# Stored attention outputs in a pool of their own, and the last batch's low halves on VectorE, in a three-stage attention and mixture kernel

## The chip, the cores and the metric

The kernel runs on one core of one Trainium2 chip. The metric is the device time of one execution in microseconds (us). A core has TensorE (PE, matmuls and transposes), VectorE (DVE), ScalarE (ACT), GpSimd (POOL) and SyncE (SP), which here only issues DMA transfers. Each engine runs its own instructions in their order and waits at semaphores for the others. The profile shows the TensorE clock as the share of full speed that was granted.

## The reference

Three blocks follow each other for 8 batches of 576 tokens, 512 features wide, all in float32.

```
phi(x)  = [exp(xw - max|xw|), exp(-(xw - max|xw|))]         # xw = x @ w_phi, per head
attn    = phi(q) @ (phi(k)^T @ v) / (phi(q) @ sum(phi(k)))  # 8 heads of 64
# mixture: 4 experts, the best 2 of 4 by gate logits, weights by softmax
y      += w_e * softmax(causal(q_e k_e^T / 8)) v_e @ wo_e
# second mixture block, x_prev is x one token earlier
xk, xr  = mu_k x + (1 - mu_k) x_prev,  mu_r x + (1 - mu_r) x_prev
out     = sigmoid(xr @ w_r) * ((relu(xk @ w_k)^2) @ w_v)
```

## The kernel before

**Number form.** A float32 matrix product is made of three matmuls in a reduced form (fp32r): each operand is split into a high half (a rounded copy, on ACT) and a low half (operand minus high half, on DVE or POOL); the products are high x high, high x low and low x high. `split` (lines 95 to 100; the subtraction is line 100) and `mm3` do that.

**Stages.** `favors` makes the attention of all batches into the buffer XT. `moe1` takes a batch from XT, makes queries, keys, values and gates, and runs the causal attention of 4 experts in tasks of 128 queries: scores, softmax (POOL's scaling is line 558), transposes, product with the values (`av_task`, tile yp, summed into `yf`). After two experts, `taps` (lines 611 to 622) makes the *stored attention output* of that batch and half: `dl` is the difference of neighbouring tokens, and the tile `yt` holds high and low halves of the even tokens (288 columns) and of the differences (576 columns). ACT makes the high halves, `el` the low ones, and SP stores all of it (864 KB) to `yd` in DRAM. So `taps` runs 16 times.

`gates_keys` reads `yd` back in 6 chunks of 768 tokens and multiplies it by weights that were composed with `wo` beforehand (`compose`; its results pass through a tile in the same buffer as `yt`): 36 units a chunk, 6 matmuls each (tile rk), evacuated by ACT or DVE, stored to `kd`. The weights of a unit (tile wt, 256 KB) are loaded by SP into one of 5 buffers, asked for when the unit four places earlier is evacuated.

`moe2` is the last product. It reads a chunk of `kd` as four blocks b11, b12, b21, b22 and makes it in 7 products instead of 8 (the sums T1 = b12 - b11, T2 = b22 - T1, T3 = b22 - b12, T4 = b21 - T2). Each block is split into one of three slots of XT, then 24 matmuls follow (tile vacc, two halves of 12). `post` gathers the products: the third and fourth are kept as `u2` and `u4` until the sixth and seventh, and the gates (tile zs, sigmoid on ACT) multiply the output.

**Order.** `weave` interleaves the streams and a scheduler sets each engine's order when the kernel is built. The first `weave` ends with `moe1`; then the pools of that stage are closed (`phA.close()`), and the PSUM pool psB and the SBUF pool pB of the last stage are opened. Pools at the right side lie on each other as in a stack: XT, pQ (four weight tiles, used again as buffers later), then pA, and after pA is closed, pB in the room that pA had. A tile of pB waits until the tiles of pA that lay there are no longer read or written. The first two products of chunk 0 (b11, b21) need nothing of pB: their blocks are loaded to XT and pQ and split there by `first`. The raw b11 stays in `wqh` and `wql`, and b12 and b22 in XT, until lines 866 to 869 make the sums from them in pB.

The condition in line 618 asks for a key 'pW' in `state`; the code puts 'pW' in `late` alone, so `el` is POOL for all 16.

Of the kernel before, what the change touches and what calls it, by code (L numbers as in the profile page):

```python
# [6 lines left out]
F32 = mybir.dt.float32  # L7
F32R = mybir.dt.float32r
# [5 lines left out]
P = 128  # L14
B, S, H, D = (8, 576, 8, 64)
# [8 lines left out]
HP_ = S // 2  # L24
HC = CH // 2
# [51 lines left out]
def fused_kernel(ctx: ExitStack, tc: tile.TileContext, qT, kT, vx, wphi, wq, wk, wvg, wo, mu, w64, ident, cmask, tri, out):  # L77
# [14 lines left out]
    def eng(c):  # L92
        return {'v': nc.vector, 'p': nc.gpsimd}[c]
# [13 lines left out]
    state = {}  # L107
# [16 lines left out]
    XT = pX.tile([P, 16 * S], F32R, name='XT')  # L124
    pQ = ctx.enter_context(tc.tile_pool(name='pQ', bufs=1, side='right'))
    wqh, wql, wkh, wkl = (pQ.tile([P, 2, 4, P], F32R, name=n) for n in ('wqh', 'wql', 'wkh', 'wkl'))
    pA = phA.enter_context(tc.tile_pool(name='pA', bufs=1, side='right'))
    phF = ExitStack()
    pF = phF.enter_context(tc.tile_pool(name='pF', bufs=1))
# [77 lines left out]
    def compose():  # L207
        sw = [pR.tile([P, 4, 256], F32R, name='sw', tag=f'y{h}') for h in range(2)]
        for i in range(2):
            st_ = pR.tile([P, 2, 256], F32, name='wof', tag='e', bufs=4)  # L210
            nc.sync.dma_start(st_, wo[:, 2 * i:2 * i + 2])
            split(sw[0][:, 2 * i:2 * i + 2], sw[1][:, 2 * i:2 * i + 2], st_)
            yield 1
        for u in range(12):
            wth, wtl = ([pR.tile([P, 2, 2, P], F32R, name=n, tag='w', bufs=NWB) for _ in range(2)] for n in ('wth', 'wtl'))
            for hf in range(2):
                hz = (yield from decode(pF, 2 * u + hf, dict(tag='e', bufs=4), 'a', pool_raw=pR))
                hz = hz.rearrange('p (k n) -> p k n', k=2)
                a_ = pF.tile([P, 2, P], F32, name='ma', tag='dr')
                for k in range(2):  # L220
                    nc.vector.tensor_scalar(a_[:, k], hz[:, k], mus[:, int(u < 4), 2 * hf + k:2 * hf + k + 1], None, op0=OP.mult)
                split(wth[hf][:, :, 0], wtl[hf][:, :, 0], hz, 'a', nc.gpsimd)
                yield 1
                split(wth[hf][:, :, 1], wtl[hf][:, :, 1], a_, 'a', nc.gpsimd)
                yield 1
            ps = psK.tile([P, 512], F32, name='fo', tag='rk')
            for ep in range(2):
                es = slice(ep * P, ep * P + P)
                mm3(ps[:, ep * 256:ep * 256 + 256], [(sw[0][:, kt, es], sw[1][:, kt, es], wth[kt // 2][:, kt % 2].rearrange('p x n -> p (x n)'), wtl[kt // 2][:, kt % 2].rearrange('p x n -> p (x n)')) for kt in range(4)])
                yield 1  # L230
            f_ = pF.tile([P, 2, 2, P], F32, name='cb', tag='pm', bufs=3)
            o = pA.tile([P, 2, 3, 2, P], F32R, name='wo_', tag='yt')
            p4 = ps.rearrange('p (e x n) -> p e x n', e=2, x=2)
            evac('a', f_[:, 0], p4[:, :, 0])
            oh, ol = (o[:, h].rearrange('p x e n -> p e x n')[:, :, 0::2] for h in range(2))
            evac('a', oh, p4)
            nc.vector.tensor_sub(f_[:, 1], p4[:, :, 1], f_[:, 0])
            nc.vector.tensor_sub(ol, p4, oh.bitcast(F32))
            split(o[:, 0, 1], o[:, 1, 1], f_[:, 1], 'a', nc.gpsimd)
            nc.sync.dma_start(wf[u], o.bitcast(F32))  # L240
            yield 1
        state['composed'] = True
# [174 lines left out]
    def moe1():  # L417
# [167 lines left out]
        def av_task(b, e, hf):  # L585
            ep, j = (e // 2, e % 2)
            W = 256 if hf == 0 else 320
            q0 = 256 * hf
            d = {}
            hr = slice(64 * j, 64 * j + 64)  # L590

            def mm():
                ps = psA.tile([P, 320], F32, name='yp', **tg('yp'))
                hi, lo = (x.rearrange('p (k q) -> p k q', q=W) for x in AT[b, e, hf])
                nk = 2 if hf == 0 else 5
                cost = 0
                for pa, (cw, src) in enumerate(((P, hi), (64, lo))):
                    for k in range(nk):
                        o = max(0, P * k - q0)
                        nc.tensor.matmul(ps[:cw, o:W], VS[b][:, k, e, :cw], src[:, k, o:W], start=pa == 0 and k == 0, stop=pa == 1 and k == nk - 1, skip_group_check=True)  # L600
                        cost += max((W - o) / 2.4, cw / 1.2)
                d['ps'] = ps
                return cost

            def ev():
                ps = d['ps']
                yc = pA.tile([64, 320], F32, name='yc', tag='a', bufs=3)
                evac('a', yc[:, :W], ps[64:P, :W])
                nc.vector.tensor_add(YF[ep][hr, 1 + q0:1 + q0 + W], ps[0:64, :W], yc[:, :W])

            def taps():
                if not (j == 1 and hf == 1):
                    return
                yf = YF[ep]
                dl = pA.tile([P, S], F32, name='dl', tag='a', bufs=3)
                nc.vector.tensor_sub(dl, yf[:, 1:], yf[:, 0:S])
                yt = pA.tile([P, 2, 3, HP_], F32R, name='yt', tag='yt')
                el = eng('v' if 'pW' in state else 'p')
                split(yt[:, 0, 0], yt[:, 1, 0], yf[:, 1:].rearrange('p (t two) -> p two t', two=2)[:, 0], 'a', el)
                split(yt[:, 0, 1:], yt[:, 1, 1:], dl.rearrange('p (t two) -> p two t', two=2), 'a', el)  # L620
                nc.sync.dma_start(yd[b][:, :, ep], yt.bitcast(F32))
                stored[b] = stored.get(b, 0) + 1
            return [mm, ev, taps]
# [169 lines left out]
    late = {}  # L793

    def moe2():
# [33 lines left out]
        def chunk(c):  # L829
            pB = late['pB']  # L830
            d = {}

            def load(*names):

                def go():
                    for n in names:
                        if n == 'w2':
                            d[n] = combo(2, 0, 2, pB, pB, 1536, 'kx', 8)
                        elif n[0] == 'w':
                            d[n] = home(int(n[1]), *((wkh, wkl) if n == 'w5' else (wqh, wql)))  # L840
                        elif n[0] == 'g':
                            d[n] = pB.tile([P, 4, HC], F32, name='zs', tag='zs', bufs=2)
                            nc.sync.dma_start(d[n], kd[c][:, 0:4, int(n[1])])
                        elif n[0] == 'b':
                            d[n] = pB.tile([P, 4, HC], F32, name='kx', tag='kx', bufs=8)
                            nc.sync.dma_start(d[n], block(c, *src[n], 0, 4))
                return (lambda: done.get(c, 0) >= (NB if 'g0' in names else 24), go)
# [60 lines left out]
            def post(j):  # L908
# [7 lines left out]
                def tmp(tag, bufs):  # L916
                    return pB.tile([P, HC], F32, name='t', tag=tag, bufs=bufs)

                def go():
                    for dp in range(2):  # L920
                        x, y, w = (d.get((k, dp)) for k in 'xyw')
                        g = lambda par, r: d[f'g{par}'][:, 2 * dp + r]
                        if j == 0:
                            d['z', dp] = tmp('t', 3)
                            evac('a', d['z', dp], x)
                        elif j == 1:
                            nc.vector.tensor_add(out_(dp, 0)[:, 0], y, d['z', dp])
                        elif j == 2:
                            d['u2', dp] = tmp('u2', 2)
                            evac('a', d['u2', dp], x)  # L930
                        elif j == 3:
                            d['u4', dp] = tmp('u4', 2)
                            evac('a', d['u4', dp], x)
                        elif j == 4:
                            o = out_(dp, 0)[:, 0]
                            nc.vector.tensor_mul(o, o, g(0, 0))
                            nc.vector.tensor_mul(out_(dp, 0)[:, 1], x, g(1, 0))
                            store(dp, 0)
                        else:
                            t = tmp('t', 3)  # L940
                            nc.vector.tensor_add(t, w, d['u4' if j == 5 else 'u2', dp])
                            nc.vector.tensor_mul(out_(dp, 1)[:, 6 - j], t, g(6 - j, 1))
                            if j == 6:
                                store(dp, 1)
# [84 lines left out]
```

## Time and profile before

| | |
|---|---|
| median of 3 runs | 1256.39 us (1253.61 to 1257.29) |
| profiled execution | 1252.4 us, span 1250.4 us |
| mean granted clock | 0.992 |
| PE busy | 1210.9 us (97%) |
| DVE busy | 938.9 us (75%) |
| ACT busy | 817.9 us (65%) |
| POOL busy | 434.2 us (35%) |
| chain that ended last | PE 81%, DVE 7%, DMA 4%, ACT 3% |

PE is busy nearly all the time, so the profile is read for the stretches in which it is not. In the page's strip of forty slices of 31 us the PE share is under nine tenths in four slices (the first, those from 813 and 1000 us on, and the last), and the granted clock in two of them (the first, and the one from 1000 us on). "Idle before" at a row of an engine names the time that it stood still and what released it.

### The profile page before, as it was taken

What the parts mean: (1) busy time and instruction counts of PE and PEld (TensorE: products, weight loads), DVE (VectorE), ACT (ScalarE), POOL (GpSimd) and SP (SyncE); (2) the same over time, 40 slices, a digit from 0 to 9 for tenths busy, and PEclk for the clock granted to TensorE, in tenths of its full rate; (3) what the DMA queues carried; (4) which work ended last, traced back from release to release, by engine and by line L of the source; (5) the groups of instructions that cost most, each with busy time, mean ns of one, the idle gap of its engine ahead of it and who ended that gap; (6) DMA issues with size and microseconds to landing.
All of it is one profiled execution on the core that took longest, in us unless ns stands there. A gap on an engine that the chain in (4) does not pass through costs nothing.

```text
span 1250.4 us, 26664 instructions
## 1 busy us (share of the span) xinstructions
PE 1210.9 (97%) x9014; PEld 1169.7 (94%) x9014; DVE 938.9 (75%) x2489; ACT 817.9 (65%) x2008; POOL 434.2 (35%) x634
## 2 busy tenths in 40 slices
PE   8999999999999999999999999989999989999998
PEld 7899899999999999999999999988898879999998
DVE  7875988888977777787788678747667577767765
ACT  6665767677767776776668667568577575456533
POOL 5542666445633334553544543333113200000000
PEclk8999999999999999999999999999999989999999
DMA  6322134322226444454555434755798988798753
GB/s 203 93 88 85 62 103 149 109 71 80 101 96 181 131 133 118 114 172 137 150 141 185 127 118 125 221 197 171 231 296 265 324 295 284 247 315 300 270 192 127
DMA packets 186918, 212.70 MB, mean 170 GB/s; under 512 B 34464, under 2 KB 170528, under 8 KB 186784
## 3 DMA queue, kind: packets, MB, share of 16 engines
q1 hardware_dynamic: 172960, 192.12, 49.2%
q10 hardware_dynamic: 13824, 18.88, 4.2%
q8 instruction: 73, 1.20, 0.4%
q14 instruction: 61, 0.50, 0.1%
HBM read 145.94 MB, written 65.01 MB: 169 GB/s over the span
## 4 chain that ended last, share of the span: by engine, by line
PE 81%; DVE 7%; DMA 4%; ACT 3%; issue 2%; POOL 2%; SPq 0%; POOLq 0%; ACTq 0%; DVEq 0%
PE rk L117 16%; PE vacc L903 13%; PE kv L342 9%; PE num L385 8%; PE qk L117 6%; PE vp L117 4%; PE yp L600 3%; PE at L565 3%; PE pj L287 3%; PE pj L288 2%; PE pj L289 2%; PE tq L369 2%; PE fo L117 2%; PE sc L527 2%; PE sc L528 2%
## 5 line engine op out<-in xcount | busy, mean ns | idle before, releaser
L558 POOL TENSOR_SCALAR a<-a,sv,gw 128x128 f32<-128x128 f32 (+4 forms) x160 | 108.1, 677 | 222.8 <-DVE sv L552 79.6
L100 POOL TENSOR_TENSOR lo<-raw,hi 128x256 fp32r<-128x256 f32 (+1 forms) x160 | 110.0, 690 | 180.5 <-ACT hi L97 167.6
L385 PE MATMUL num<-kvs,ph 128*128 128x65 f32 (+1 forms) x1280 | 142.2, 262 | 0.6 <-DVE xs L392 0.6
L385 PEld LDWEIGHTS num<-kvs,ph 128*128 128x128 f32 (+1 forms) x1280 | 137.2, 181 | 4.5 <-issue 1.3
L903 PE MATMUL vacc<-XT,wch 128*128 128x384 f32 x480 | 124.2, 337 | 2.6 <-DVE XT L100 2.5
L297 DVE TENSOR_REDUCE m<-pj 128x4 f32<-128x512 f32 (+1 forms) x160 | 100.8, 631 | 34.1 <-PE pj L289 32.8
L547 ACT ACTIVATE a<-sc,sv 128x128 f32<-128x128 f32 (+2 forms) x192 | 98.1, 513 | 20.5 <-DVE sv L542 11.5
L740 DVE TENSOR_TENSOR z<-rk,z 128x384 f32<-128x384 f32 x144 | 79.1, 551 | 36.0 <-PE rk L117 29.5
L299 DVE TENSOR_TENSOR pm<-pj,m 128x512 f32<-128x512 f32 (+1 forms) x160 | 100.2, 630 | 4.6 <-ACT ph L323 2.0
L100 DVE TENSOR_TENSOR XT<-kx,XT 128x1536 fp32r<-128x1536 f32 x40 | 70.2, 1754 | 31.7 <-ACT XT L97 31.6
L542 DVE TENSOR_REDUCE sv<-sc 128x1 f32<-128x128 f32 (+2 forms) x192 | 88.6, 469 | 5.0 <-PE sc L528 2.0
L287 PE MATMUL pj<-wph,hi 128*128 128x256 f32 x288 | 89.9, 312 | 2.3 <-ACT hi L97 1.0
L903 PEld LDWEIGHTS vacc<-XT,wch 128*128 128x128 f32 x480 | 87.6, 190 | 3.2 <-DVE XT L100 2.8
L97 ACT ACTIVATE XT<-kx 128x1536 fp32r<-128x1536 f32 x40 | 59.5, 1487 | 37.2 <-PE vacc L903 30.2
L289 PE MATMUL pj<-wph,lo 128*128 128x256 f32 x288 | 82.4, 286 | 0.6 <-POOL lo L100 0.6
L97 ACT ACTIVATE hi<-raw 128x256 fp32r<-128x256 f32 (+1 forms) x160 | 62.0, 392 | 31.4 <-PE pj L288 9.5
L288 PE MATMUL pj<-wpl,hi 128*128 128x256 f32 x288 | 81.7, 284 | 0.0
L903 PE MATMUL vacc<-XT,wcl 128*128 128x384 f32 x240 | 80.4, 336 | 0.0
L565 PE MATMUL at<-idn,a 128*128 128x128 f32 (+2 forms) x480 | 72.9, 261 | 4.9 <-POOL a L558 4.6
L742 ACT ACTIVATE z<-z 128x384 f32<-128x384 f32 x96 | 49.7, 521 | 33.2 <-DVE z L740 28.0
L582 DVE TENSOR_TENSOR at1l<-at,at1h 128x384 fp32r<-128x384 f32 (+3 forms) x128 | 59.2, 462 | 15.5 <-ACT at1h L581 13.3
L581 ACT ACTIVATE at1h<-at 128x384 fp32r<-128x384 f32 (+3 forms) x128 | 53.4, 418 | 22.3 <-PE at L565 15.4
(528 smaller groups left out, 3694.8 us busy)
## 6 DMA issues: line engine op xcount, KB each, us to landing
wt<-wf SPq DMA_DIRECT2D x216, 256.0 KB, 3.7
kd<-z ACTq DMA_DIRECT2D x96, 192.0 KB, 3.5
kx<-kd SPq DMA_DIRECT2D x21, 768.0 KB, 8.1
yd<-yt SPq DMA_DIRECT2D x16, 864.0 KB, 4.7
kd<-z SPq DMA_DIRECT2D x48, 192.0 KB, 4.3
zs<-kd SPq DMA_DIRECT2D x12, 768.0 KB, 6.4
out_dram<-o SPq DMA_DIRECT2D x24, 384.0 KB, 3.2
raw<-in_kT_dram SPq DMA_DIRECT2D x64, 128.0 KB, 2.5
```

Of the source, the lines that this page charges most:

```text
L97: nc.scalar.activation(hi, src, AF.Copy)
L100: (el or nc.vector).tensor_sub(lo, src, hi.bitcast(F32))
L117: nc.tensor.matmul(ps, a, m, start=first and i == 0, stop=last and i == n - 1)
L287: nc.tensor.matmul(o, hi[:, c], wph, start=True, stop=False)
L288: nc.tensor.matmul(o, hi[:, c], wpl, start=False, stop=False)
L289: nc.tensor.matmul(o, lo[:, c], wph, start=False, stop=True)
L297: nc.vector.tensor_reduce(m[:, :g], ps, axis=AX.X, op=OP.max, apply_absolute_value=True)
L342: nc.tensor.matmul(bank[:, r, :], d['kp'][:, r % 2, c0:c0 + P], v, start=new and r == 0, stop=end, skip_group_check=True)
L385: nc.tensor.matmul(ps[lo_:hi_, i, j, :], d['qp'][:, hf, c0 + lo_:c0 + hi_], kvs[hp, b][:, r * 65:(r + 1) * 65], start=hf == 0, stop=hf == 1)
L558: eng(asc).tensor_scalar(a[:m, :nk], a[:m, :nk], rc[:m], WT[b][:m, i, e:e + 1], op0=OP.mult, op1=OP.mult)
L565: nc.tensor.transpose(ps[:kw, jj * m:jj * m + m], d['a'][:m, jj * P:jj * P + kw], idn[:m, :m])
L903: nc.tensor.matmul(ps, a[:, f, dp], m[:, f], start=j in (0, 1, 5) and n == 0, stop=n == 11, skip_group_check=True)
```

## The change

There are three edits. A pool pY is opened at the right side between pQ and pA, and it stays to the end; `yt`, and the tile of `compose` that shares its buffer, move there from pA. The engine of the low halves is DVE for the last batch (two of the 16 times) and POOL else. In the last stage, `u2` and `u4`, which were tiles of pB with two buffers each, become the four quarters of one tile `u` in pY, in the buffer that `yt` had.

```diff
--- before.py
+++ after.py
@@ -124,6 +124,7 @@
     XT = pX.tile([P, 16 * S], F32R, name='XT')
     pQ = ctx.enter_context(tc.tile_pool(name='pQ', bufs=1, side='right'))
     wqh, wql, wkh, wkl = (pQ.tile([P, 2, 4, P], F32R, name=n) for n in ('wqh', 'wql', 'wkh', 'wkl'))
+    pY = ctx.enter_context(tc.tile_pool(name='pY', bufs=1, side='right'))
     pA = phA.enter_context(tc.tile_pool(name='pA', bufs=1, side='right'))
     phF = ExitStack()
     pF = phF.enter_context(tc.tile_pool(name='pF', bufs=1))
@@ -229,7 +230,7 @@
                 mm3(ps[:, ep * 256:ep * 256 + 256], [(sw[0][:, kt, es], sw[1][:, kt, es], wth[kt // 2][:, kt % 2].rearrange('p x n -> p (x n)'), wtl[kt // 2][:, kt % 2].rearrange('p x n -> p (x n)')) for kt in range(4)])
                 yield 1
             f_ = pF.tile([P, 2, 2, P], F32, name='cb', tag='pm', bufs=3)
-            o = pA.tile([P, 2, 3, 2, P], F32R, name='wo_', tag='yt')
+            o = pY.tile([P, 2, 3, 2, P], F32R, name='wo_', tag='yt')
             p4 = ps.rearrange('p (e x n) -> p e x n', e=2, x=2)
             evac('a', f_[:, 0], p4[:, :, 0])
             oh, ol = (o[:, h].rearrange('p x e n -> p e x n')[:, :, 0::2] for h in range(2))
@@ -614,8 +615,8 @@
                 yf = YF[ep]
                 dl = pA.tile([P, S], F32, name='dl', tag='a', bufs=3)
                 nc.vector.tensor_sub(dl, yf[:, 1:], yf[:, 0:S])
-                yt = pA.tile([P, 2, 3, HP_], F32R, name='yt', tag='yt')
-                el = eng('v' if 'pW' in state else 'p')
+                yt = pY.tile([P, 2, 3, HP_], F32R, name='yt', tag='yt')
+                el = eng('v' if b == B - 1 else 'p')
                 split(yt[:, 0, 0], yt[:, 1, 0], yf[:, 1:].rearrange('p (t two) -> p two t', two=2)[:, 0], 'a', el)
                 split(yt[:, 0, 1:], yt[:, 1, 1:], dl.rearrange('p (t two) -> p two t', two=2), 'a', el)
                 nc.sync.dma_start(yd[b][:, :, ep], yt.bitcast(F32))
@@ -830,6 +831,11 @@
             pB = late['pB']
             d = {}
 
+            def kept(n):
+                if 'kept' not in late:
+                    late['kept'] = pY.tile([P, 4, HC], F32, name='u', tag='yt')
+                return late['kept'][:, n]
+
             def load(*names):
 
                 def go():
@@ -926,10 +932,10 @@
                         elif j == 1:
                             nc.vector.tensor_add(out_(dp, 0)[:, 0], y, d['z', dp])
                         elif j == 2:
-                            d['u2', dp] = tmp('u2', 2)
+                            d['u2', dp] = kept(dp)
                             evac('a', d['u2', dp], x)
                         elif j == 3:
-                            d['u4', dp] = tmp('u4', 2)
+                            d['u4', dp] = kept(2 + dp)
                             evac('a', d['u4', dp], x)
                         elif j == 4:
                             o = out_(dp, 0)[:, 0]
```

The scheduler makes a new order from about 960 us on; up to there all engines have the same order. In the rows below, a number behind a name tells tiles of one name apart, brackets hold the semaphores that are waited for (DMAHW is that of a DMA, Pool that of POOL, Activation that of ACT), and line numbers behind the first edit are 1 higher, behind the fourth 6 higher.

DVE at the change of stage, before: kx_15798 is T1, kx_15799 T2, kx_15800 T3, kx_15801 the copy of b22; a row with XT and two inputs makes a low half.

```order
L616 TENSOR_TENSOR dl_15698<-yf1_141 128x576 [waits DVE_49,Pool_49]
L866 TENSOR_TENSOR kx_15798<-XT_105,wqh_109 128x768 [waits DMAHW7_49,DMAHW2_49,Pool_49]
L866 TENSOR_TENSOR kx_15798<-XT_105,wql_110 128x768
L927 TENSOR_TENSOR o_15881<-vacc_15811,t_15807 128x384 [waits PE_49,Activation_49]
L927 TENSOR_TENSOR o_15883<-vacc_15824,t_15809 128x384 [waits PE_49,Activation_49]
L867 TENSOR_TENSOR kx_15799<-XT_105,kx_15798 128x1536 [waits DVE_49]
L869 TENSOR_TENSOR kx_15800<-XT_105 128x1536
L100 TENSOR_TENSOR XT_105<-kx_15798,XT_105 128x1536 [waits Activation_49]
L740 TENSOR_TENSOR z_14850<-rk_14809,z_14794 128x384 [waits DMAHW3_49,PE_49]
L740 TENSOR_TENSOR z_14864<-rk_14857,z_14805 128x384 [waits DMAHW4_49,PE_49,Activation_49]
L936 TENSOR_TENSOR o_15881<-o_15881,zs_15981 128x384 [waits DVE_49,Activation_49]
L936 TENSOR_TENSOR o_15883<-o_15883,zs_15981 128x384 [waits DVE_49]
```

DVE at the same place now: kx_15801 is T1, kx_15802 T2, kx_15803 T3, kx_15804 the copy of b22.

```order
L617 TENSOR_TENSOR dl_15701<-yf1_144 128x576 [waits DVE_49]
L100 TENSOR_TENSOR yt_15703<-yf1_144,yt_15703 128x288 [waits Activation_49]
L100 TENSOR_TENSOR yt_15703<-dl_15701,yt_15703 128x576 [waits Activation_49]
L872 TENSOR_TENSOR kx_15801<-XT_105,wqh_109 128x768 [waits DVE_49,Pool_49]
L872 TENSOR_TENSOR kx_15801<-XT_105,wql_110 128x768
L873 TENSOR_TENSOR kx_15802<-XT_105,kx_15801 128x1536 [waits DVE_49]
L875 TENSOR_TENSOR kx_15803<-XT_105 128x1536
L933 TENSOR_TENSOR o_15884<-vacc_15814,t_15810 128x384 [waits PE_49,Activation_49]
L100 TENSOR_TENSOR XT_105<-kx_15801,XT_105 128x1536 [waits Activation_49]
L933 TENSOR_TENSOR o_15886<-vacc_15827,t_15812 128x384 [waits PE_49]
L100 TENSOR_TENSOR XT_105<-kx_15802,XT_105 128x1536 [waits Activation_49]
```

The two low halves of `yt` stand ahead of the first sum now, which waits for no DMA semaphore, and the low halves of T1 and T2 come ahead of the evacuations of rk.

ACT at the change of stage, before: line 104 evacuates (t of moe2, z of rk), line 97 makes high halves, line 856 is the sigmoid of the gates.

```order
L104 ACTIVATE t_15807<-vacc_15736 128x384 [waits DMAHW2_49,PE_49,Pool_49]
L104 ACTIVATE t_15809<-vacc_15749 128x384 [waits PE_49]
L97 ACTIVATE XT_105<-kx_15798 128x1536 [waits DVE_49]
L868 ACTIVATE kx_15801<-XT_105 128x1536
L104 ACTIVATE z_14805<-rk_14798 128x384 [waits PE_49]
L856 ACT_TABLE_LOAD
L856 ACTIVATE zs_15981<-zs_15981 128x1536 [waits DMAHW3_49]
L97 ACTIVATE XT_105<-kx_15801 128x1536 [waits Activation_49]
L856 ACTIVATE zs_15983<-zs_15983 128x1536 [waits DMAHW4_49]
L97 ACTIVATE XT_105<-kx_15799 128x1536 [waits DVE_49]
L97 ACTIVATE wqh_109<-wql_110 128x1024 [waits DMAHW5_49]
```

ACT at the same place now:

```order
L104 ACTIVATE t_15810<-vacc_15739 128x384 [waits DVE_49,PE_49,Pool_49]
L874 ACTIVATE kx_15804<-XT_105 128x1536
L104 ACTIVATE t_15812<-vacc_15752 128x384 [waits PE_49]
L97 ACTIVATE XT_105<-kx_15801 128x1536 [waits DVE_49]
L97 ACTIVATE XT_105<-kx_15802 128x1536 [waits DVE_49]
L97 ACTIVATE XT_105<-kx_15804 128x1536 [waits PE_49,Activation_49]
L862 ACT_TABLE_LOAD
L862 ACTIVATE zs_15983<-zs_15983 128x1536 [waits DMAHW3_49]
L104 ACTIVATE z_14808<-rk_14801 128x384 [waits PE_49]
L862 ACTIVATE zs_15985<-zs_15985 128x1536 [waits DMAHW4_49]
L97 ACTIVATE wqh_109<-wql_110 128x1024 [waits DMAHW5_49]
L743 ACTIVATE z_14853<-z_14853 128x384 [waits DVE_49]
```

The high halves of T1, T2 and b22 stand ahead of the sigmoids now, and the first row waits for DVE instead of a DMA semaphore.

PE behind the first two products, before: rk are units of `gates_keys`, wch3 is the weight of the T2 block.

```order
L903 MATMUL vacc_15824<-XT_105,wch1_13327 128x384 x2
L903 MATMUL vacc_15824<-XT_105,wcl1_13328 128x384
L117 MATMUL rk_14798<-yc__14550,wt_14713 128x384 x6
L117 MATMUL rk_14809<-yc__14595,wt_14727 128x384 x6
L117 MATMUL rk_14857<-yc__14595,wt_14747 128x384 x6
L117 MATMUL rk_14871<-yc__14628,wt_14796 128x384 x6
L117 MATMUL rk_14885<-yc__14628,wt_14807 128x384 x6
L903 MATMUL vacc_15736<-XT_105,wch3_13447 128x384
```

PE at the same place now:

```order
L909 MATMUL vacc_15827<-XT_105,wch1_13330 128x384 x2
L909 MATMUL vacc_15827<-XT_105,wcl1_13331 128x384
L117 MATMUL rk_14801<-yc__14553,wt_14716 128x384 x6
L117 MATMUL rk_14812<-yc__14598,wt_14730 128x384 x6
L909 MATMUL vacc_15739<-XT_105,wch3_13450 128x384
L909 MATMUL vacc_15752<-XT_105,wch3_13450 128x384
```

Two rk units are left ahead of the T2 block where five stood; the other three come later. In SP's queue the first gate load, right behind the last store of `yt`, waited for that store's semaphore and now waits for POOL instead.

## Rows read from the trace of the kernel before

**Rows 1.** PE, DVE, ACT busy by stretch; count of instructions; granted clock, DMA share, GB/s.

```profile
1001.43:1020.68 19.25, 13.12 (x55) 11.85 (x55) 16.68 (x17) 16.14 (x19) 0.00 (x0) 0.82 1.05 367
1020.68:1245.50 224.82, 224.80 (x1297) 224.48 (x1296) 154.78 (x175) 114.66 (x148) 0.00 (x0) 1.00 0.74 247
```

**Rows 2.** The chain that ended last: start us, us, what.

```profile
1215.15 30.35 PE vacc L903 x175
```

**Rows 3.** PE in order of time: start us, us, what, idle before.

```profile
1001.43 1.20 PE L117 MATMUL rk<-yc__14550,wt 128*128 128x384 f32 x6
1002.47 1.21 PE L117 MATMUL rk<-yc__14595,wt 128*128 128x384 f32 x6
1005.43 1.33 PE L117 MATMUL rk<-yc__14595,wt 128*128 128x384 f32 x6 [1.76 <-ACT z L104]
1008.57 3.69 PE L117 MATMUL rk<-yc__14628,wt 128*128 128x384 f32 x12 [1.81 <-DVE z L740]
1012.35 0.62 PE L903 MATMUL vacc<-XT,wch 128*128 128x384 f32 x2
...
1015.43 0.69 PE L903 MATMUL vacc<-XT,wch 128*128 128x384 f32 x1 [2.47 <-DVE XT L100]
```

**Rows 4.** Busy by stretch again, in 3 us stretches, columns as in the first group.

```profile
1009.00:1012.00 3.00, 3.00 (x12) 2.94 (x11) 3.00 (x4) 3.00 (x3) 0.00 (x0) 0.58 1.05 388
...
1015.00:1018.00 3.00, 2.57 (x8) 2.57 (x9) 3.00 (x4) 2.02 (x6) 0.00 (x0) 0.50 1.09 354
```

**Rows 5.** DVE in order of time, the change of stage.

```profile
992.50 0.75 DVE L616 TENSOR_TENSOR dl<-yf 128x576 f32<-128x576 f32 x1
1000.28 0.96 DVE L866 TENSOR_TENSOR kx<-XT,wqh 128x768 f32<-128x768 f32 x1 [7.03 <-issue]
1001.15 0.95 DVE L866 TENSOR_TENSOR kx<-XT,wql 128x768 f32<-128x768 f32 x1
1002.02 1.02 DVE L927 TENSOR_TENSOR o<-vacc,t 128x384 f32<-128x384 f32 x2
...
1004.62 1.75 DVE L869 TENSOR_TENSOR kx<-XT 128x1536 f32<-128x1536 f32 x1
...
1013.63 1.75 DVE L100 TENSOR_TENSOR XT<-kx,XT 128x1536 fp32r<-128x1536 f32 x1
```

**Rows 6.** ACT in order of time, the change of stage.

```profile
993.28 0.74 ACT L97 ACTIVATE yt<-dl 128x576 fp32r<-128x576 f32 x1
...
1000.30 0.87 ACT L104 ACTIVATE t<-vacc 128x384 f32<-128x384 f32 x2 [5.35 <-DMA yd<-yt]
...
1003.53 1.47 ACT L868 ACTIVATE kx<-XT 128x1536 f32<-128x1536 f32 x1
...
1005.39 1.28 ACT L856 ACT_TABLE_LOAD   x1
...
1010.82 1.47 ACT L97 ACTIVATE XT<-kx 128x1536 fp32r<-128x1536 f32 x1
```

**Rows 7.** SP queue in order of time, the change of stage.

```profile
995.59 0.56 SPq L621 DMA_DIRECT2D yd<-yt  x1
1000.25 0.92 SPq L843 DMA_DIRECT2D zs<-kd  x2
```

**Rows 8.** Instructions on tile dl: duration ns min/median/max, first and last start.

```profile
L616 DVE TENSOR_TENSOR dl<-yf x16: 748/760/1358, 184.6 to 992.5; 128x576 f32<-128x576 f32 x16
```

**Rows 9.** Tile zs, 990 to 1030 us: its two loads.

```profile
DMA to landing us min/median/max: 4.4/5.2/6.0
```

**Rows 10.** All engines in order of time, 967 to 971 us.

```profile
967.47 1.45 POOL L100 TENSOR_TENSOR yt<-dl,yt 128x576 fp32r<-128x576 f32 x1
...
967.87 1.07 DVE L544 TENSOR_TENSOR sv<-sv 64x1 f32<-64x1 f32 x1
...
970.68 0.82 POOL L558 TENSOR_SCALAR a<-a,sv,gw 64x576 f32<-64x576 f32 x1 [1.75 <-ACT at1h L581]
```

**Rows 11.** Line 544 from 900 to 1000 us, columns as for tile dl.

```profile
L544 DVE TENSOR_TENSOR sv<-sv x4: 142/151/1068, 935.1 to 983.0; 64x1 f32<-64x1 f32 x4
```

## The prediction

> **What bounds the kernel now.** I read the busy table by stretches first. From 1020.68 to 1245.50 us TensorE (PE) is busy 224.80 of 224.82 us at a granted clock of 1.00: nothing off PE can shorten that stretch, and it holds a fixed number of matmuls. The stretch just ahead, 1001.43 to 1020.68, is the opposite: 13.12 us busy of 19.25, granted clock 0.82, while VectorE (DVE) and ScalarE (ACT) are busy 16.68 and 16.14 us [rows 1]. The chain that ended last gives the price of a matmul at full rate: 175 in 30.35 us, 0.1734 us each [rows 2].
>
> PE's rows in order of time show what goes wrong: three idle gaps, 1.76, 1.81 and 2.47 us, released by ACT, DVE and DVE, and rows that take too long for their count, such as 12 matmuls in 3.69 us [rows 3]. The granted clock there is 0.58 and 0.50 in the stretches 1009 to 1012 and 1015 to 1018, the lower of the two levels (1.2 GHz), after the first two gaps and again after the third [rows 4].
>
> Why are DVE and ACT late? DVE ends `dl` at 993.25 and then stands still for 7.03 us in front of line 866, the first sum of moe2 [rows 5]. ACT stands still too, 5.35 us, and its row names the releaser: the DMA from yt to yd [rows 6]. SP issued that store at 995.59, after GpSimd (POOL) had made the low halves, and its next issue, the gate load zs, comes only at 1000.25 [rows 7]. So three engines wait for one store of 864 KB, because the pool pB of the last stage takes the room in which yt lies. PE has 48 ready matmuls to cover it, from 993.1 to 1001.4, and then runs dry.
>
> **What the stretch costs.** Between 1001.43 and 1020.68 PE does five rk units of 6 matmuls and one block of 24, 54 in all [rows 3]. At 0.1734 us they need 9.36 us; they took 19.25. Lost: 9.89 us, of which 1.76 + 1.81 + 2.47 = 6.04 us idle, and 3.85 us at the low clock. This is the most that the change can win here.
>
> On the low clock the Trainium skill ("TensorE: Matmul & The Clock Gate", Part 1) says that for modelling the ramp is under 1% of a kernel's span and not worth fitting. By that rule the sum would have only the idle time, 6.0 us before what remains. The rows disagree for this purpose: 3.85 us is 0.3% of the span indeed, but it is four tenths of what is at stake, so I count it.
>
> **Part 1: yt in a pool of its own.** In the new order the first sum (line 872 now) waits for DVE's own earlier work and for POOL, and for no DMA; ACT's first evacuation and SP's gate load lose the same wait. What they still wait for in POOL is the scaling of the last attention tile, done long before (it ends before PE's last attention matmuls). I follow the new order with durations of before, and PE as before up to 1001.43, since its 48 matmuls wait for nothing that changes.
>
> DVE: `dl` ends 993.25 [rows 5]; the small low half (288 columns, about 0.4 us by half of `dl`'s 0.75) until 993.7; the large one waits for ACT's high half, which ends at 994.02 [rows 6], then takes 0.75 like `dl` (576 columns, two operands; 748 ns at least in 16 runs [rows 8]): 994.8. Then the two halves of T1 in steps of 0.87 (1000.28 to 1001.15 to 1002.02), to 996.5; T2 and T3 at about 1.7 each [rows 5], to 999.9. One output sum of 0.5 to 1000.4; T1's low half, 1.7, to 1002.1; the other output sum, which waits for PE's 48th matmul at 1001.4, to 1002.6; T2's low half, 1.75 [rows 5], to **1004.3**. Before, it ended at 1013.63 + 1.75 = 1015.4.
>
> ACT: the first evacuation of a sum runs at 995.0; b22's copy (1.47), the second evacuation and T1's high half (1.47) are done by 999.1; T2's high half waits for T3, which reads the slot it goes to, and ends at 999.9 + 1.5 = 1001.4. Then b22's high half to 1002.9, the table load to 1004.2 [rows 6], two sigmoids (1.4 each, the size of b22's copy) with an rk evacuation (0.4) between them to 1007.4, `wqh` (1024 columns for 1536, 1.0) to 1008.4, a Relu and the copy to `u` (0.45 each) to 1009.3.
>
> PE: two rk units instead of five stand ahead of the T2 block now, to 1001.43 + 12 x 0.1734 = 1003.5; two matmuls with T2's high half to 1003.9; then a wait for the low half until 1004.3: **0.4 us** instead of 6.04. 22 matmuls to 1008.1, two rk units to 1010.2, and then the block of T1 needs `u` free on ACT's side: 1009.3, so 0.9 us to spare. With gaps this short the clock has no cause to fall as after the 1.8 us gaps. The three rk units moved behind cost PE the same 18 matmuls there.
>
> SP: the store is issued at about 994.9, the gate loads right behind it at 995.5 instead of 1000.25. They landed 4.4 to 6.0 us after issue [rows 9], so by 1001.5, and the first sigmoid wants them at 1004.2. `wql` and the kx loads follow 5.4 us earlier as well. Cover enough; if it were gone, the sigmoids would push `u`, and each us beyond 0.9 would be one of PE.
>
> **Part 2: the last batch's low halves on DVE.** Two pairs, one at about 965 and the one above: 0.4 + 0.75 = 1.15 us more DVE work each. At 967.47 POOL's large low half takes 1.45 us, and a 64x1 sum of DVE started at 967.87 ends with it, after 1.07 us [rows 10] where its kind takes 0.14 at least [rows 11]. So the pair gives DVE back about 0.9 us and costs it 1.15. PE had rk units to run there and I price the difference at 0; bounds, minus 1 and plus 1.2 us.
>
> The Trainium skill ("SBUF — State Buffer", Who interferes with whom) says that a DVE operation with two SBUF inputs and a POOL operation that reads SBUF exclude each other, whoever starts first. By it the moved pair could itself be blocked by POOL's next scaling: that would make the sum 0.8 us worse (the scaling of 64x576 at 970.68 [rows 10]). The trace agrees on the exclusion (1.07 us); at the second pair POOL has nothing left to run.
>
> **Part 3: u2 and u4 as one tile of four quarters.** Two buffers of each were there before, so no buffer is lost; the new waits in front of the copies name the matmul just finished, as before. Price 0. The remaining stage keeps its 1297 matmuls. It is ordered anew, since the scheduler starts from another state; PE had no gap there in 225 us. I take 0; the bounds are 0 and 5.4 us, three moved rk units each with the 1.8 us that an rk unit waited at worst [rows 3].
>
> **Sum.** -9.89 + 0.4 + 0 + 0 = -9.5, I take -9.4. The profiled execution, 1252.4 us (span 1250.4), would become 1243.0. It lies 4.0 us under the median of the runs shown (1256.39), so the median becomes **1247.0 us**. About 0.3% (3.8 us) is what a measurement of this kernel can tell from no change.
>
> **Rivals.**
> *The gap shrinks but the clock falls all the same.* DVE's path to T2's low half is a chain of seven operations in which each can slip. If PE waits 2.0 us rather than 0.4 and the block of 24 runs slow as before (22 matmuls from 1015.43 to 1020.68, 5.25 us instead of 3.81), 3.4 us of the 9.9 stay: gain 6.4, 1250 us. For it: DVE and ACT are the busy ones there. Against: their work is done 5.5 us earlier, and 48 matmuls cover it.
>
> *The wait only changes its name.* The new pB lies over other tiles of pA, and one may be freed as late as the store was: gain near 0, 1256 us. Against: the order names only DVE and POOL now, and POOL has finished.
>
> *Slower.* SP issues in order. In the new order three kx loads and one gate load (768 KB each) stand ahead of rk weights which stood ahead of some of them before. 3.1 MB at 367 GB/s [rows 1] is 8.6 us. A weight is asked for about 60 matmuls (10.4 us) before its use; so from the point where its own landing takes over 1.8 us more behind those loads, PE waits. If each weight behind such a group lands 5 us late at three chunks, 15 us are lost with the clock falling besides: 9.4 gained, 15 lost, 1262 us. For it: DMA share is 1.05 in the stretch. Against: over the rest it is 0.74 [rows 1], and PE never waited for a weight there.
>
> **How the numbers follow.** Forecast as summed 0.74, small gain 0.12, no effect 0.07, slower 0.07. The forecast's own spread is 1.2 us of part 2 and about 2 of the runs: 1243 to 1250. With the small gain the range 1243 to 1253 holds about 0.84. Faster: 0.74 + 0.12 less 0.02 = 0.84; within the bound 0.09; slower 0.07.
>
> **What would show it.** Right: line 872 starts at about 994.8 in place of 1000.28, the gate loads right behind the store; two rk units and then the T2 block with a gap under 1 us; clock 1.00 in the stretch after 1001; PE full after it until the end. Wrong: a gap over 1.5 us ahead of the T2 block or the T1 block, a clock under 0.9, or PE gaps after 1020.

## The result: 9 us gained at the change of stage

The changed kernel takes 1243.27 us (median of 6 runs, 1241.64 to 1247.39) against 1254.60 us (6 runs, 1252.09 to 1257.29). The ratio is 0.9913, with an interval of 0.9891 to 0.9935: 10.9 us, between 8.2 and 13.7. The forecast was 1247.0 us, in a range of 1243 to 1253; the median lies in the range by 0.27 us. The kernel before has another median here than in the forecast (1254.60 in 6 runs, 1256.39 in 3). The profiled execution of the changed kernel took 1247.39 us, the longest of its six; its span is 1245.4.

In the rows below the first sum is L872 (L866 before) and the `vacc` matmuls are L909 (L903).

PE of the changed kernel in order of time, from the end of the 48 matmuls (start us, us, what, idle before); the answer to [rows 3]:

```profile
1005.55 1.20 PE L117 MATMUL rk<-yc__14553,wt 128*128 128x384 f32 x6
1006.59 1.20 PE L117 MATMUL rk<-yc__14598,wt 128*128 128x384 f32 x6
...
1008.88 0.44 PE L909 MATMUL vacc<-XT,wch 128*128 128x384 f32 x1 [0.73 <-DVE XT L100]
...
1012.82 1.20 PE L117 MATMUL rk<-yc__14598,wt 128*128 128x384 f32 x6
1013.86 1.20 PE L117 MATMUL rk<-yc__14631,wt 128*128 128x384 f32 x6
```

One gap of 0.73 us is left of three that summed to 6.04. The busy time by stretch shows the rest; the first row is as long as the first of [rows 1], from the same instruction on (PE, PEld, DVE, ACT, POOL busy; granted clock, DMA share, GB/s):

```profile
1005.55:1024.80 19.25, 18.52 (x106) 18.17 (x106) 14.79 (x15) 16.46 (x22) 0.00 (x0) 1.00 1.06 380
1024.80:1240.50 215.70, 215.70 (x1246) 215.66 (x1245) 152.98 (x174) 110.16 (x143) 0.00 (x0) 1.00 0.75 254
```

PE does 106 matmuls where it did 55, at a clock of 1.00 instead of 0.82, and stays full to the end. The releasers have changed on DVE and on SP; their rows answer to [rows 5] and [rows 7]. DVE in order of time:

```profile
996.86 0.75 DVE L617 TENSOR_TENSOR dl<-yf 128x576 f32<-128x576 f32 x1
...
998.41 0.76 DVE L100 TENSOR_TENSOR yt<-dl,yt 128x576 fp32r<-128x576 f32 x1 [0.43 <-ACT yt L97]
999.27 0.96 DVE L872 TENSOR_TENSOR kx<-XT,wqh 128x768 f32<-128x768 f32 x1
...
1007.07 1.75 DVE L100 TENSOR_TENSOR XT<-kx,XT 128x1536 fp32r<-128x1536 f32 x1
```

The SP queue:

```profile
999.19 0.56 SPq L622 DMA_DIRECT2D yd<-yt  x1
999.84 1.98 SPq L849 DMA_DIRECT2D zs<-kd  x2
```

The first sum starts 0.08 us after the start of the store instead of 4.69 us, and the gate loads stand right behind it.

**One measure for all kernels.** I call "the stage" the time from the first rk unit behind the 48 matmuls to the end of the span. Before it was 1250.4 - 1001.43 = 248.97 us, after 1245.4 - 1005.55 = 239.85: **9.12 us shorter**, where the working had 9.5. The end of the span is the landing of the last output store, which the change doesn't touch and which varies too. PE's last matmul, before and after:

```profile
1245.15 0.34 PE L903 MATMUL vacc<-XT,wcl 128*128 128x384 f32 x1
1240.44 0.34 PE L909 MATMUL vacc<-XT,wcl 128*128 128x384 f32 x1
```

From its start to the end of the span it is 5.25 us before and 4.96 after; so up to PE's last matmul the stage went from 243.72 to 234.89 us, 8.83 us less.

The spans differ by 5.0 only, because this execution came to the stage 4.12 us later. Most of that loss lies far ahead, where no instruction had moved: between the starts of two of ACT's high halves of `dl`, at 235.76 and 318.70 us, it took 82.94 us against 79.79 in the kernel before (235.85 to 315.64), and in between lies the stretch 270 to 280 us. Of the changed kernel, columns as above:

```profile
270.00:280.00 10.00, 10.00 (x59) 10.00 (x60) 6.52 (x17) 5.74 (x19) 5.26 (x7) 0.66 0.33 109
```

Of the kernel before:

```profile
270.00:280.00 10.00, 9.93 (x85) 9.93 (x86) 7.27 (x22) 8.85 (x25) 5.97 (x8) 1.00 0.36 124
```

59 matmuls at a clock of 0.66 against 85 at 1.00, and PE is never idle in it. Whether this dip belongs to the changed kernel is the first question below.

### The profile page after: what moved, and what is told of

It reads as the page before. It is cut to its first block, busy times and chain, and to the rows that moved or that the text cites. A ratio compares the mean times of both kernels' runs of the same rounds, so it can differ in the third digit from the quotient of the medians.

```text
span 1245.4 us, 26673 instructions
## 1 busy us (share of the span) xinstructions
PE 1209.5 (97%) x9014; PEld 1169.1 (94%) x9014; DVE 943.0 (76%) x2493; ACT 817.4 (66%) x2008; POOL 428.3 (34%) x630
## 4 chain that ended last, share of the span: by engine, by line
PE 81%; DVE 8%; DMA 4%; ACT 3%; POOL 2%; issue 2%; SPq 0%; POOLq 0%; ACTq 0%; DVEq 0%
PE rk L117 16%; PE vacc L909 13%; PE kv L343 10%; PE num L386 8%; PE qk L117 6%; PE vp L117 4%; PE yp L601 3%; PE at L566 3%; PE pj L288 3%; PE pj L290 2%; PE pj L289 2%; PE fo L117 2%; PE tq L370 2%; PE sc L528 2%; PE sc L529 2%
## 5 line engine op out<-in xcount | busy, mean ns | idle before, releaser
L909 PE MATMUL vacc<-XT,wch 128*128 128x384 f32 x480 | 123.3, 334 | 0.7 <-DVE XT L100 0.7
L909 PEld LDWEIGHTS vacc<-XT,wch 128*128 128x128 f32 x480 | 86.8, 188 | 1.1 <-DVE XT L100 1.1
L909 PE MATMUL vacc<-XT,wcl 128*128 128x384 f32 x240 | 79.6, 334 | 0.0
```

The lines of the kernel that those rows point to most:

```text
L909: nc.tensor.matmul(ps, a[:, f, dp], m[:, f], start=j in (0, 1, 5) and n == 0, stop=n == 11, skip_group_check=True)
```

## The experiments

Each is compared with runs of the kernel before on the same chip; those had medians of 1253.65 us for the kernels from "changed, again" to "T2 split in halves", 1254.47 for the four after them and 1254.79 for the last. "Stage" is from the one profiled execution of each, and so are the two columns behind it.

| kernel | median us | ratio to before, interval | stage us | up to PE's last matmul | sum of PE's gaps around the T2 block |
|---|---|---|---|---|---|
| before | 1254.60 | | 248.97 | 243.72 | 6.04 |
| changed | 1243.27 | 0.9913 (0.9891 to 0.9935) | 239.85 | 234.89 | 0.73 |
| changed, again | 1245.30 | 0.9937 (0.9914 to 0.9961) | 239.79 | 234.83 | 0.73 |
| pool alone | 1251.34 | 0.9976 (0.9958 to 0.9994) | 245.34 | 239.42 | 3.48 |
| low halves alone | 1253.91 | 0.9996 (0.9977 to 1.0014) | 247.44 | 242.46 | 5.60 |
| T2 split in halves | 1243.06 | 0.9907 (0.9884 to 0.9931) | 238.88 | 234.00 | 0 |
| late by 0.5 us, order changes | 1249.24 | 0.9966 (0.9951 to 0.9981) | 244.37 | 239.47 | 3.48 |
| late by 1 us, order kept | 1249.18 | 0.9958 (0.9944 to 0.9973) | 240.83 | 235.88 | 1.76 |
| last pair alone on DVE | 1246.66 | 0.9937 (0.9918 to 0.9955) | 239.82 | 234.85 | 0.73 |
| before, gap filled | 1251.45 | 0.9988 (0.9971 to 1.0005) | 247.33 | 242.42 | 3.78 |
| all sixteen pairs on DVE | 1265.70 | 1.0095 (1.0068 to 1.0122) | not comparable | | |

**The changed kernel again.** No edit.

> The changed kernel once more, unaltered, for a second trace of it. Theory (the store's wait and the low clock behind it were worth 9.1 us, and the rest of the 11.3 us between the medians is spread of the runs): from the start of the last rk units ahead of the T2 block to the end of the span 239.9 us again, within 0.3, and the stretch 270 to 280 us at a granted clock of 1.00 instead of 0.72 and 0.60, with the stage change then about 4 us earlier. Rival (the dip at 270 to 280 us belongs to the changed kernel): the dip is there again at the same place and the stage change stands at 1005.5.

The stage is 1243.4 - 1003.61 = 239.79 us, and the dip is gone; its row of the same stretch:

```profile
270.00:280.00 10.00, 8.86 (x76) 8.87 (x77) 7.98 (x26) 8.73 (x25) 5.24 (x7) 1.00 0.26 79
```

The dip is not a mark of the changed kernel: of the ten profiled executions of kernels with this part alike (all but the last of the table) three have it, the changed kernel once and not the second time. Between the same two high halves of `dl` it takes 79.74 us now, 3.2 less than with the dip. The stage change came 1.94 us earlier, not 4, since other stretches vary too. So the medians carry some us of such chance each, and the stage is the sharper measure.

**The pool alone.**

```
-                el = eng('v' if b == B - 1 else 'p')
+                el = eng('p')
```

> yt in its own pool, but all low halves on POOL as before. Theory (the pool alone is the gain): the first sum L872 no longer waits for the store; it waits for POOL's large low half, so it starts about 2.2 to 2.3 us after dl's end instead of 1.66 in the changed kernel and 7.0 in the kernel before. The order has four rk units ahead of the T2 block's third matmul instead of two, so PE's gap there is under 0.7. From the first rk unit behind the 48 matmuls to the end 239.5 to 240.5 us; in all 0.5 us from the changed kernel either way: 1243 to 1244. Rival (the low halves on DVE bring the gain): most of the 9 us is gone, 1250 or more.

The theory failed. The first sum behaved as expected; DVE's row:

```profile
1000.92 0.96 DVE L872 TENSOR_TENSOR kx<-XT,wqh 128x768 f32<-128x768 f32 x1 [2.33 <-POOL yt L100]
```

But of the 9.1 us only 3.6 came (of the 8.83 up to PE's last matmul 4.30; the last store took 1 us longer to land here). PE in order of time:

```profile
1007.71 1.20 PE L117 MATMUL rk<-yc__14598,wt 128*128 128x384 f32 x6
1009.84 0.62 PE L909 MATMUL vacc<-XT,wch 128*128 128x384 f32 x2 [0.93 <-ACT XT L97]
1013.01 1.94 PE L117 MATMUL rk<-yc__14598,wt 128*128 128x384 f32 x6 [2.55 <-ACT z L104]
1014.74 2.12 PE L117 MATMUL rk<-yc__14631,wt 128*128 128x384 f32 x6
1016.66 0.42 PE L909 MATMUL vacc<-XT,wch 128*128 128x384 f32 x1
```

The two rk units that were to cover the T2 block stand in front of its third matmul on an engine that works in order, and the first of them waits for ACT's copy of an earlier rk result. ACT in order of time:

```profile
1006.92 2.86 ACT L97 ACTIVATE XT<-kx 128x1536 fp32r<-128x1536 f32 x2 [0.97 <-PE vacc L909]
1009.80 1.28 ACT L862 ACT_TABLE_LOAD   x1
1011.10 1.48 ACT L862 ACTIVATE zs<-zs 128x1536 f32<-128x1536 f32 x1
1012.49 0.47 ACT L104 ACTIVATE z<-rk 128x384 f32<-128x384 f32 x1
```

DVE had T2's low half done at 1010.48; the block went on at 1016.66. Up to PE's last matmul this kernel is 4.53 us behind the changed one: 2.75 us are more idle time, and most of the rest is the low clock behind the long gap, where an rk unit takes 1.94 and 2.12 us. Columns as in [rows 1]:

```profile
1014.66:1016.66 2.00, 2.00 (x7) 2.00 (x7) 2.00 (x3) 1.97 (x4) 0.00 (x0) 0.50 1.07 376
```

**The low halves alone.** The kernel before with only this line changed:

```
-                el = eng('v' if 'pW' in state else 'p')
+                el = eng('v' if b == B - 1 else 'p')
```

> The last batch's low halves on DVE, but yt in the old pool, so that the first sum still waits for the store. Theory (store): the store is issued about 0.7 us earlier and so the first sum starts 0.7 us earlier; PE's order through the T2 block is that of before, with gaps that sum to 5 to 6 us and a granted clock near 0.82 in that stretch; time 0.5 to 1 us below the kernel before, not to be told from it. Rival (low halves): 1243 to 1246, 9 us below.

The wait for the store is there as before, now under the DMA's own name:

```profile
1003.24 0.96 DVE L866 TENSOR_TENSOR kx<-XT,wqh 128x768 f32<-128x768 f32 x1 [5.27 <-DMA yd<-yt]
```

From `dl` (995.67) to the store's issue (998.00) it took 2.33 us instead of 3.09, but the landing took 0.55 us more, so the first sum gained 0.2 us, not 0.7. The gaps sum to 5.60 us; the time can't be told from before. The stage is 1.5 us shorter (1.26 up to PE's last matmul), but the edit can't be credited with it. PE's rows:

```profile
1004.36 1.20 PE L117 MATMUL rk<-yc__14550,wt 128*128 128x384 f32 x6
1018.40 0.45 PE L903 MATMUL vacc<-XT,wch 128*128 128x384 f32 x1 [2.02 <-DVE XT L100]
1022.36 1.89 PE L117 MATMUL rk<-yc__14550,wt 128*128 128x384 f32 x10
```

The T2 block goes on 14.04 us after the stage begins, as in the kernel before (14.00). Only its 22 matmuls are faster, 3.96 us instead of 5.25, at a higher clock; the kernel before with its gap filled, further down, shows the same without this edit. Up to PE's last matmul, pool alone gives 4.30, low halves alone 1.26 at most, both together 8.83: the parts don't add.

**T2 split in halves.**

```
-                        split(*slot(7 * c + j), d[ops[j]], 'a')
+                        [split(*(x[:, f] for x in slot(7 * c + j)), d[ops[j]][:, f], 'a') for f in ((slice(0, 2), slice(2, 4)) if (c, j) == (0, 2) else (slice(0, 4),))]
```

> The changed kernel with T2's split in two halves of 768 columns, on ACT and on DVE, so that the T2 block can begin with the first. Theory (the 0.73 us of PE in front of the T2 block is the last that the wait has left, since DVE's T2 low half of 1.75 us ends it): the first half ends 0.85 us earlier, the gap is under 0.1 us, 0.5 to 0.7 us less from the stage change to the end (239.2 us); in the median not to be told from the changed kernel. Rival (something behind DVE, ACT or the u copy, takes its place): the same 239.9 with another wait in front of the next block.

PE has no gap any more:

```profile
1003.96 1.20 PE L117 MATMUL rk<-yc__14598,wt 128*128 128x384 f32 x6
1005.00 0.83 PE L909 MATMUL vacc<-XT,wch 128*128 128x384 f32 x3
```

The stage is 0.9 to 1.0 us shorter than the changed kernel's, a little more than the gap. It is the shortest stage of all; its median, 1243.06, can't be told from 1243.27.

**Late by half a us, so that the order changes.** Added behind the line that makes the tiles of T1, T2, T3 and b22:

```
+                        nc.vector.tensor_sub(d['T1'][:, 0:1], raw['b12'][:, 0:1], raw['b11', 0][:, 0:1])
```

> The changed kernel with one useless DVE subtraction of 384 columns (about 0.5 us) ahead of the first sum. The order that comes out has four rk units ahead of the T2 block instead of two, as with the low halves on POOL (1251.3 us). Theory (the order is the price: the third and fourth rk unit wait for a bank that ACT empties only behind the table load and a sigmoid): PE waits 2 to 3 us for ACT's copy z of rk with the granted clock falling behind it, and from the first rk unit behind the 48 matmuls to the end it takes 244 to 246 us instead of 239.8. Rival (only lateness of DVE counts): 239.8 plus 0.5, 240.3 us.

PE shows the same picture as the pool alone, though POOL has no low half here:

```profile
1004.31 0.62 PE L909 MATMUL vacc<-XT,wch 128*128 128x384 f32 x2 [0.93 <-ACT XT L97]
1007.48 1.74 PE L117 MATMUL rk<-yc__14598,wt 128*128 128x384 f32 x6 [2.55 <-ACT z L104]
```

An instruction of 0.56 us costs 4.5 us of stage. Up to PE's last matmul it is 4.58, and with the pool alone 4.53: two causes of lateness, one order, one price.

**Late by a us, with the order kept.** Added at the same place, behind the line that makes `scr`:

```
+                        [nc.gpsimd.tensor_sub(scr, raw['b22'][:, i], raw['b12'][:, i]) for i in range(2)]
```

> The changed kernel with two useless POOL subtractions of 384 columns beside DVE's first sums, which delay DVE where both read SBUF; the order of PE and DVE through the T2 block is that of the changed kernel, two rk units ahead. Theory (order): DVE's T2 low half ends 0.5 to 2 us later than in the changed kernel, PE's gap in front of the T2 block grows from 0.73 by just that, and the stage is 240.3 to 242 us, short of the 245.3 of the kernel with POOL's low halves although DVE is at least as late. Rival (lateness alone made that loss): 245 us.

`scr` is a tile of its own that nothing reads. POOL's two subtractions and DVE's sums got in each other's way, and the order stayed that of the changed kernel. POOL's row:

```profile
999.81 3.41 POOL L869 TENSOR_TENSOR scr<-XT 128x384 f32<-128x384 f32 x2 [8.95 <-issue]
```

DVE's rows (0.95 and 1.76 us in the changed kernel):

```profile
1000.57 1.77 DVE L872 TENSOR_TENSOR kx<-XT,wql 128x768 f32<-128x768 f32 x1
1002.38 2.46 DVE L873 TENSOR_TENSOR kx<-XT,kx 128x1536 f32<-128x1536 f32 x1
```

PE's one gap:

```profile
1010.82 0.44 PE L909 MATMUL vacc<-XT,wch 128*128 128x384 f32 x1 [1.76 <-DVE XT L100]
```

The gap grew by 1.03 us, the stage by 1.0. T2's low half ended 4.29 us after the stage began (1009.02 + 1.74 - 1006.47), later than with the pool alone (1010.48 - 1006.66 = 3.82), yet up to PE's last matmul the stage is 3.54 us shorter. The order is the price, not the lateness. (The median, 1249.18, lies higher than this stage says; its profiled execution had the dip at 270 to 280 us.)

**Only the last pair on DVE.**

```
-                el = eng('v' if b == B - 1 else 'p')
+                el = eng('v' if b == B - 1 and ep else 'p')
```

> The changed kernel with only the very last pair of low halves on DVE, the pair before it (at about 970 us) back on POOL. Theory (of the two pairs only the last sets the first sum and the order of PE): order and time of the stage as in the changed kernel, 239.8 us within 0.4; up to 970 us DVE is blocked again where POOL makes the low half, and PE comes to the stage change within 0.4 us of the changed kernel; median 1243 to 1246. Rival (the earlier pair is a part of the gain): 2 us or more above it.

```profile
1007.12 1.20 PE L117 MATMUL rk<-yc__14598,wt 128*128 128x384 f32 x6
1009.40 0.44 PE L909 MATMUL vacc<-XT,wch 128*128 128x384 f32 x1 [0.73 <-DVE XT L100]
```

PE's rows above and its stage are those of the changed kernel: of the two pairs, only the last one counts there. The median, 1246.66, lies a little above the 1243 to 1246 expected and is not to be told from the changed kernel's, whose two sets gave 1243.27 and 1245.30. PE came to the stage 0.5 and 2.5 us later than in those two executions, which themselves lie 1.94 apart, so that part of the expectation can't be judged.

**Before, with the gap filled.** Added ahead of the block's own matmuls, where the kernel names their bank:

```
+ [nc.tensor.matmul(d['y', i % 2], wh[:, 0, 0], h[:, 0], start=True, stop=True, skip_group_check=True) for i in range(8 if c == 0 and j == 2 else 0)]
```

> The kernel before with eight useless matmuls ahead of its T2 block, where PE stands idle 2.47 us for DVE's T2 low half; their results are never read. Idle time is filled, not removed. Theory A (the low clock is a cost of its own behind an idle PE, and of the 3.85 us only what lies behind the last wait is lost, since all before it is set by DVE): the idle in front of the T2 block goes to under 0.3 us, the 22 matmuls behind it take 3.8 to 4.2 us instead of 5.25, and the stage is 1.0 to 1.4 us shorter, 247.6 to 248.0 instead of 248.97. Theory B (as the prediction added it, every us at the low clock is lost for itself): the low clock in front of the T2 block is lost as well, so filling its idle can't give more than A, and 3.85 us in all would need all three gaps filled. Rival C (the clock falls for another reason than PE's idle): the 22 matmuls take 5.25 us again.

PE in order of time:

```profile
1007.73 4.13 PE L117 MATMUL rk<-yc__14628,wt 128*128 128x384 f32 x12 [1.01 <-DVE z L740]
1011.70 1.55 PE L895 MATMUL vacc<-XT,wch 128*128 128x384 f32 x8
...
1014.60 0.45 PE L903 MATMUL vacc<-XT,wch 128*128 128x384 f32 x1 [0.99 <-DVE XT L100]
...
1018.52 2.24 PE L117 MATMUL rk<-yc__14550,wt 128*128 128x384 f32 x12
```

Inconclusive on the clock. The 22 matmuls took 1018.52 - 1014.60 = 3.92 us instead of 5.25, as A says, and 0.99 us of idle stayed. But with the low halves alone, where nothing was filled and PE waited 2.02 us, they took 3.96 us too. So the filling can't be credited with it. What both show: the T2 block goes on 14.03 (1014.60 - 1000.57) and 14.04 us after the stage begins, as in the kernel before (1015.43 - 1001.43 = 14.00), however PE spent the time ahead. DVE sets that moment: in all three, the wait that ends there is for its low half.

**All sixteen pairs on DVE.**

```
-                el = eng('v' if b == B - 1 else 'p')
+                el = eng('v')
```

> The changed kernel with the low halves of all sixteen pairs on DVE instead of the last two. Theory (a pair costs DVE 1.15 us and gives it back about 0.9 that POOL took from it where both read SBUF, and in the stretch 285 to 955 us PE, busy 98 percent of it, sets the time): the stretch up to 955 us moves by no more than 3.5 us (14 pairs of 0.25), the stage at the end keeps its 239.8 us; median 1242 to 1249. Rival (DVE sets much of the batch loop, and each pair costs its 1.15): 14 pairs cost 10 us or more, 1254 or above.

The theory missed by far, the rival named the right side, and neither names the cause. DVE's last `dl` comes at 1025.5 us instead of 994.9 in the changed kernel's second trace; at the end of the span 18 of these 31 us are left (1261.7 against 1243.4). PE's order is another one throughout, and the four rk units ahead of the T2 block are back, with this row among its waits (engine, line, waited for: us in total, times, longest):

```profile
PE rk L117 <- ACT z L104: 2.9, 2, 2.6
```

How much of the 18 us is DVE's work and how much is order stays open.

That u2 and u4 share one tile was not tried by itself; its price of 0 in the prediction is not shown apart from the other two edits.

## Why the prediction was right, and where it was not

**What bounds the kernel** was right: the stage before held the loss, and the stretch behind it stayed full. That the median came out 3.7 us under the forecast and still in its range is chance in part: the forecast stood on 1256.39 us for the kernel before, and six runs gave 1254.60. The stage is the better test: 9.5 us forecast, 9.12 measured (8.83 up to PE's last matmul).

**Part 1** was right in the changed kernel. L872 was forecast for 994.8; it started at 999.27, and `dl` had come 4.36 us later than before, so 994.9. T2's low half was to end at 1004.3; it ended at 1008.82, less 4.12 us 1004.7. So the gap is 0.73 us and not 0.4, and the sum 9.1 and not 9.5. ACT's first copy to `u` was in time (1013.27, block at 1014.90), and the clock did not fall. It stayed at 1.00 also behind the one gap of 1.76 us of the kernel that is late by a us (1.00 from 1010.82 to 1014.77), so a gap as long as the first of the kernel before need not bring it down.

**Part 2's price of 0 is the step that failed.** I priced DVE's time alone, at most 1.2 us either way. In DVE's time it was near: at the first pair `dl` (968.67) took 0.75 us, where before (964.75) it took 1.18 beside POOL. That pair seems to cost a little all the same: from the high half of its `dl` to that of the last `dl` it takes 28.1 to 28.9 us in the six traces that have this one pair more on DVE, and 27.2 to 27.6 in the four that have it on POOL. That is within the bound of 1.2; what makes it was not looked into. What the price left out is the order. The last pair on POOL makes the first sum start later, and at half a us of lateness the scheduler puts four rk units instead of two ahead of the T2 block's third matmul, of which the third waits for ACT: 4.5 us up to PE's last matmul (5.5 of stage, with the longer landing of the last store). For the pool alone I did expect 1243 to 1244 us, and it took 1251.34. I had read the order only for the kernel with all parts in it.

**"6.04 idle and 3.85 at the low clock"** is a right sum of two terms that don't stand for themselves. DVE let the T2 block go on 14.0 us after the stage began; what PE lost at the low clock ahead of that, 2.4 us, would have been idle time otherwise. Only the 22 matmuls behind it, 5.25 us for 3.81, lost 1.44 on their own, and they did so in the kernel before, not in the two variants with the same wait. There is one trace of the kernel before; if most of its executions run these matmuls as the two variants do (3.92 and 3.96 us), about 1.3 us of the 9.1 belong to this execution and not to the change.

The Trainium skill ("TensorE: Matmul & The Clock Gate", Part 1) says of the ramp that for modelling its penalty is under 1% of a typical kernel span and that it is not to be fitted to a count of cold matmuls. With no term for the clock, the sum would have been 6.0 less 0.4, 5.6 us. The stage gained 9.12, so leaving it out would have misled here, because an engine at the low clock hid waiting time that the idle rows don't show.

**Rivals.** The small gain did not come with the change. Pool alone gives a gain of that kind, 4.3 us with the clock down, but by PE's order and not, as the rival had it, by slips in DVE's chain. The wait's new name is real in one respect: DVE waits for the store no more, and the 0.73 us left is DVE's own work; the split in halves took it away. The slower case did not come: in the stage of the changed kernel PE waits for no weight.

## What to carry to other kernels

When the order comes from a scheduler, price each part of a change by the order it makes, with that part left out and put in: here half a us on one engine flipped which work stood at the head of another, at 4.5 us. Work put in front as cover is cover only if it is itself ready; look at who empties its buffer. And where executions differ by several us in stretches that the change doesn't touch, compare the time from a common instruction on.

## What the runs showed of the hardware

The granted clock was well under 1.00 from 270 to 280 us in three of ten executions: 0.66, 0.66 and 0.64, with PE busy for 10.00, 9.91 and 9.35 us and 59, 58 and 52 matmuls done, against 76 to 88 in the seven at 1.00. Just ahead PE had the same two gaps of about 0.5 and 1.2 us (at 266 to 272 us) in executions with the dip and without; what brings it on in one and not in another was not found. DVE and POOL delayed each other where both ran subtractions on SBUF: two of 128x384 took POOL 1.61 and 1.71 us, where one of 128x576 takes it 1.43 at the least in the kernel before, and two DVE sums of 0.95 and 1.76 us took 1.77 and 2.46 beside them. The Trainium skill ("SBUF — State Buffer", Who interferes with whom) states that a DVE instruction with two SBUF inputs contends with a GpSimd instruction that reads SBUF; the numbers agree with it.
